# A decode block on one core: the loop of four attention steps begins at step 0, with eight turns, and what the first turn lacks stands in branches on a register

## The chip, the core and the metric

The kernel runs on one core of one Trainium2 chip. The metric is the device time of one execution in microseconds (us). Three runs of the kernel before gave 441.86, 442.12 and 442.27 us; the median is 442.12 us.

The core has five engines with an instruction stream each: PE (TensorE, the matmuls; PEld is its weight loads), DVE (VectorE), ACT (ScalarE), POOL (GpSimd) and SP (SyncE, which here issues DMAs). The core's 16 DMA engines carry all transfers, the fetches of instructions among them.

## The reference

A batch of 8 rows of width 1024 passes an attention layer and a gated layer, each behind a modulated layer norm. All inputs are bf16.

```python
mod = (silu(c) @ w_mod).reshape(8, 6, 1, 1024)        # sa, ca, ga, sb, cb, gb
h = layernorm(x) * (1 + ca) + sa
q = h @ wq                                            # 32 heads of 128
k, v = k_cache, v_cache                               # 8 batches x 4 kv heads x 8192 x 128, each kv head for 8 q heads
x = x + ga * (softmax(q @ k.T * 128 ** -0.5) @ v) @ wo
h = layernorm(x) * (1 + cb) + sb
gate = h @ W_gate                                     # 1024 x 3584
x = x + gb * ((gate * (gate > 0)) * (h @ W_up)) @ W_down
```

The two caches hold 32 pairs (kv head, batch) of 2 MB of K and 2 MB of V each. They are most of the 185.6 MB that the kernel reads.

## The kernel before

**Stages.** First the modulation (w_mod, four blocks of 3 MB) and the query projection (wq, four blocks of 2 MB). Then 32 attention steps, one for each pair n of kv head and batch. After every eight steps the output projection of that kv head (wo, 2 MB) is added. Last come the gate and up projections and the down projection (wd).

**Transfers.** Every block of weights, K or V is one DMA that SP issues (L780) into one SBUF buffer, `ring`, which has nine slots of 2 MB and a smaller region. The list `stream` is the order; SP issues the next block as soon as PE is done with the last block that lay in the same place (`behind`, L399). SP does nothing else until the output.

**An attention step n** has eight parts j = 0..7 (loop at L676). In part j PE transposes eight 128x128 tiles of K (`slot_transpose`, L580), and DVE (even j) or ACT (odd j) copies them to SBUF (`slot_evac`, L585). In between, PE computes scores of step n, DVE, PE and ACT the softmax of step n-1 (ACT's `Exp`), PE the product with V of step n-2, and the output of step n-3 is moved out (`pv_evac` on ACT, `pv_pick` on PE, `o_evac` and `o_keep` on DVE). So the steps are a software pipeline: step 0 has none of the work on older steps, step 1 has the softmax of step 0, and so on.

**Order and waits.** `_Graph` records each engine's operations in program order, with the operations they depend on. `number` (L116) gives each operation of a step's piece a semaphore; `waits` (L133) finds what an operation must still wait for; `emit` (L157) writes an engine's program. On PE, DVE and ACT the operations of steps 4 to 31 are a loop of seven turns of four steps (`L0, LN, L1 = 4, 4, N`); steps 0 to 3 and everything else are written out straight. In `loop` (L166) a wait whose value changes from turn to turn compares with a register that is raised once a turn. Work that only every second turn has (`odd=1`: the output projection) or that differs between even and odd turns (`o_keep`) stands in a branch on a register that holds 0 or 1 in turns. The parts of SP and POOL are written out.

Of the kernel before, what the change touches and what calls it, by code (L numbers as in the profile page):

```python
# [9 lines left out]


class _Op:
    __slots__ = ("eng", "fn", "deps", "inc", "value", "idx", "sem", "semval", "chan", "turn", "pos", "odd")

    def __init__(self, eng, fn, idx):
        self.eng = eng
        self.fn = fn
        self.deps = []
        self.inc = False
        self.value = 0  # L20
        self.idx = idx
        self.sem = None
        self.semval = 0
        self.chan = (eng,)
        self.turn = None
        self.pos = None
        self.odd = None


class _Buf:  # L30
# [9 lines left out]
class _Graph:  # L40
# [7 lines left out]
    def __init__(self):  # L48
        self.prog = {e: [] for e in ("pe", "dve", "act", "pool", "sp")}
        self.bufs = {}  # L50
        self.sems = {}
        self.piece = None
        self.nth = {}
        self.turn = None
        self.step = None
        self.odd = None

    def psum(self, *keys):
        for k in keys:
# [4 lines left out]
            self.bufs[key] = _Buf()  # L64
        return self.bufs[key]

    def begin(self, piece, odd=None):
        self.piece, self.nth, self.odd = piece, {}, odd

    def op(self, eng, fn, reads=(), writes=(), deps=()):  # L70
        o = _Op(eng, fn, len(self.prog[eng]))
        if self.piece is not None:
            self.nth[eng] = self.nth.get(eng, 0) + 1
            o.chan = (eng, self.piece, self.nth[eng])
            o.turn, o.odd, o.pos = self.turn, self.odd, (self.step, self.odd) + o.chan
# [24 lines left out]
        return o  # L100
# [12 lines left out]
            b.readers = {}  # L113
        return o

    def number(self, make):  # L116
# [12 lines left out]
        for c, n in count.items():  # L129
            if n:  # L130
                self.sems[c] = make("m_" + "_".join(str(x) for x in c))

    def waits(self, o, seen):  # L133

# [22 lines left out]
    def emit(self, eng, e, turns):  # L157
        ops = self.prog[eng]
        if not turns:
            return self.plain(ops, e)  # L160
        at = [i for i, o in enumerate(ops) if o.turn is not None]
        self.plain(ops[:at[0]], e)
        self.loop(eng, ops[at[0]:at[-1] + 1], e, turns)
        self.plain(ops[at[-1] + 1:], e)

    def loop(self, eng, ops, e, turns):  # L166
        by = [[o for o in ops if o.turn == k] for k in range(turns)]
        assert sum(len(b) for b in by) == len(ops)

        body, rest = [], list(by[1])  # L170
        for o in by[0]:
            while o.odd is None and rest[0].odd is not None:
                body.append(rest.pop(0))
            body.append(rest.pop(0) if o.odd is None else o)
        body += rest
        at = {}
        for k, b in enumerate(by):
            assert [o.pos for o in b] == [o.pos for o in body if o.odd in (None, k % 2)]
            seen = {}
            for o in b:  # L180

                for s, v in self.waits(o, seen if o.odd is None else dict(seen)):
                    at.setdefault(o.pos, {}).setdefault(id(s), (s, {}))[1][k] = v

        kinds = [lambda k: k, lambda k: k // 2, lambda k: (k + 1) // 2]
        regs = {}

        def value(vs, alone):
            k0, k1 = min(vs), max(vs)
            if vs[k0] == vs[k1]:  # L190
                return None, vs[k0]
            for i in (0, 2, 1) if alone else (0, 1, 2):
                t = kinds[i]
                by_, left = divmod(vs[k1] - vs[k0], max(1, t(k1) - t(k0)))
                first = vs[k0] - by_ * t(k0)
                if left == 0 and all(v == first + by_ * t(k) for k, v in vs.items()):
                    assert first > 0
                    return (i, by_, first), 0
            raise AssertionError(vs)

        plan = {}
        for pos, d in at.items():
            for s, vs in d.values():
                r, v = value(vs, pos[1] is None and all(k % 2 for k in vs))
                if r is not None and r not in regs:
                    regs[r] = e.alloc_register("%s_%d_%d_%d" % (eng, *r))
                    e.reg_mov(regs[r], r[2])
                plan.setdefault(pos, []).append((s, v if r is None else regs[r]))
        kind = [[r for r in regs if r[0] == i] for i in range(3)]
        odd = kind[1] or kind[2] or any(o.odd is not None for o in body)  # L210
        if odd:
            turn = e.alloc_register(eng + "_turn")
            e.reg_mov(turn, 0)

        def one(o):
            for s, v in plan.get(o.pos, ()):
                e.wait_ge(s, v)
            ins = o.fn(e)
            if o.inc:
# [4 lines left out]
                e.reg_add(regs[r], regs[r], r[1])  # L224

        with e.Fori(0, turns):
            if kind[2]:
                with e.If_eq(turn, 1):
                    add(kind[2])
# [11 lines left out]
            if kind[1]:  # L241
                with e.If_eq(turn, 1):
                    add(kind[1])
            add(kind[0])
            if odd:
                e.reg_mul(turn, turn, -1)
                e.reg_add(turn, turn, 1)


def bass_adaLN_cond__gqa_block_cached__glu_gated_reglu__decode_kernel(  # L250
# [25 lines left out]
    N = G * B  # L276
# [11 lines left out]
    with ExitStack() as es:  # L288
# [372 lines left out]
            dve("tensor_tensor", out=yR[:], in0=Y, in1=yR[:], op=ALU.add, reads=[pY, "yR"], writes=["yR"])  # L661


        def run(fn, *args, odd=None):
            g.begin("%s_%d" % (fn.__name__, j), odd)
# [8 lines left out]
        g.begin(None)  # L674

        for n in range(N + 4):  # L676
            g.turn = (n - L0) // LN if L0 <= n < L1 else None
            g.step = (n - L0) % LN
            wg = (n - 11) // B if n >= 11 and (n - 11) % B == 0 else None
            for j in range(8):  # L680
                if n < N:
# [6 lines left out]
                if 0 <= n - 3 < N:  # L688
# [3 lines left out]
                        run(pv_pick, n - 3)  # L692
                    elif j == 2:
                        run(o_evac, n - 3)
                        run(o_keep, n - 3, odd=(n - L0) // LN % 2)
                if 0 <= n - 2 < N and j % 2 == 1:
                    run(pv, n - 2, j // 2)
                if wg is not None and j in (4, 6):
                    run(wo_part, wg, 2 * j - 8, 2 * j - 4, odd=1)
                if wg is not None and j == 6:  # L700
                    run(wo_add, odd=1)
                if n >= 10 and (n - 10) % B == 0:
                    if j == 3:
                        run(re_turn, ot2[:].rearrange("p h r b -> p (h r b)"), "ot", odd=1)
                    elif j == 4:
                        run(re_spread, odd=1)
                    elif j == 6:
                        run(re_rows, otR[:], "otR", odd=1)
                if 0 <= n - 1 < N:
                    if j == 1:  # L710
                        run(soft_max, n - 1)
# [72 lines left out]
        g.number(lambda name: E(nc.semaphore(name)))  # L784

        block_ = E(nc.Block())
        engs = {"sp": (nc.sync, block_.sync), "act": (nc.scalar, block_.scalar), "pool": (nc.gpsimd, block_.gpsimd),
                "dve": (nc.vector, block_.vector), "pe": (nc.tensor, block_.tensor)}
        for name, (e, starter) in engs.items():
            def body(_, name=name, e=e):  # L790
                g.emit(name, e, (L1 - L0) // LN if name in LOOPED else 0)
                if name == "sp":
                    for o in last:
                        e.wait_ge(o.sem, o.semval)
# [29 lines left out]
```

## Time and profile before

| what | value |
|---|---|
| median of three runs | 442.12 us |
| the profiled execution | 442.3 us |
| its span in the profile | 440.5 us |
| PE, DVE, ACT busy | 75%, 44%, 41% of the span |
| bytes read, rate over the span | 185.63 MB, 421 GB/s |
| loads in the list of SP | 90 |
| instruction fetches of 16384 B (queue q8) | 11 |
| instruction fetches of 8192 B while the kernel runs (queue q14) | 5 |

The span is the time from the first to the last record of the profile; 1.8 us of the execution lie outside it. The page gives busy times by engine and in 40 slices, the DMA queues, the chain of work that ended last, and the costliest groups of instructions. The trace also holds each DMA packet with its start, its duration and its queue, and the time of every semaphore update, so that the landing of each load on each of the 16 DMA engines can be read.

### The profile page before, as it was taken

The page shows a single profiled execution, that of the slowest core. Times are in us where ns is not written, and L with a number is a line of the kernel's source. Part 1 is how long each engine was busy: PE and PEld are TensorE (multiplying, and loading weights), DVE is VectorE, ACT ScalarE, POOL GpSimd, SP SyncE. Part 2 cuts the span into 40 slices and gives each one's busy share as a digit, 9 for nine tenths or more (in the row PEclk, how much of TensorE's full clock was granted, in tenths as well). Part 3 has the DMA queues.
Part 4 walks back from the last instruction along what each step waited for, and adds up shares of the span by engine and source line. Part 5 has one row for each costly group of instructions (what it writes and reads, how often), then busy time and mean ns, then how long its engine had stood idle before and what let it go on. Part 6 is the DMA issues. An engine that isn't in the chain of part 4 may idle for free.

```text
span 440.5 us, 9704 instructions
## 1 busy us (share of the span) xinstructions
PE 329.1 (75%) x4114; PEld 203.9 (46%) x4114; DVE 193.5 (44%) x498; ACT 180.6 (41%) x235; POOL 7.5 (2%) x44
## 2 busy tenths in 40 slices
PE   1525578999888849998887599888849988753753
PEld 1102165656555526665555356555526655431221
DVE  3004044556445544554556155445544555435110
ACT  3000036566645433655654256555433645410000
POOL 1000000000000000000000000000000000000000
PEclk9998559999999997999999699999988999955755
DMA  8999999999999999999999999999999999999994
GB/s 347 435 420 430 433 430 428 427 434 427 427 430 431 431 431 431 430 431 431 430 433 433 430 431 430 434 428 431 433 430 431 431 431 434 426 427 431 426 428 183
DMA packets 13456, 185.87 MB, mean 422 GB/s; under 512 B 1488, under 2 KB 1520, under 8 KB 1920
## 3 DMA queue, kind: packets, MB, share of 16 engines
q1 hardware_dynamic: 13376, 185.61, 98.7%
q8 instruction: 11, 0.18, 0.1%
q10 hardware_dynamic: 64, 0.04, 0.1%
q14 instruction: 5, 0.04, 0.0%
HBM read 185.63 MB, written 0.02 MB: 421 GB/s over the span
## 4 chain that ended last, share of the span: by engine, by line
DMA 69%; PE 23%; DVE 4%; issue 2%; ACT 1%; SPq 1%; ACTq 0%
DMA ring<-in_A_k_cache_dram 48%; PE PS L424 13%; DMA ring<-in_A_wq_dram 11%; PE PS L420 10%; DMA ring<-in_B_W_down_dram 9%; SPq L780 1%; DVE pt L428 1%; DVE ov L428 0%; ACT ov L431 0%; DVE qT L428 0%; ACT pr L431 0%; DVE os L428 0%; DVE mp L428 0%; ACT L431 0%; DVE lh L428 0%
## 5 line engine op out<-in xcount | busy, mean ns | idle before, releaser
L431 ACT ACTIVATE KT<-PS 128x1024 bf16<-128x1024 bf16 (+1 forms) x132 | 133.4, 1011 | 209.6 <-PE PS L424 146.1
L424 PE MATMUL PS<-identb,ring 128*128 128x128 bf16 x2048 | 153.6, 225 | 34.0 <-DMA ring<-in_A_k_cache_dram 33.4
L424 PEld LDWEIGHTS PS<-identb,ring 128*128 128x128 bf16 x2048 | 124.6, 102 | 61.3 <-DMA ring<-in_A_k_cache_dram 43.6
L428 DVE COPY KT<-PS 128x1024 bf16<-128x1024 bf16 (+1 forms) x130 | 89.6, 689 | 131.7 <-PE PS L424 108.6
L420 PE MATMUL PS<-KT,qz 128*32 128x512 bf16 x512 | 52.8, 400 | 0.4 <-ACT KT L431 0.4
L420 PE MATMUL PS<-ring,pt 128*32 128x512 bf16 x512 | 50.8, 391 | 0.0
L428 DVE TENSOR_REDUCE mp<-PS 128x1 f32<-128x512 f32 x32 | 22.1, 692 | 8.6 <-PE PS L420 5.6
L431 ACT ACTIVATE pr<-PS,nb 128x512 bf16<-128x512 f32 x32 | 22.0, 687 | 7.1 <-DVE nb L428 6.5
L424 PE MATMUL PS<-identf,ov 128*128 128x128 f32 x128 | 22.8, 305 | 1.5 <-ACT ov L431 1.4
L428 DVE COPY pt<-PS 128x512 bf16<-128x512 bf16 x32 | 13.5, 423 | 22.0 <-PE PS L424 22.0
L420 PE MATMUL PS<-ring,siluT 128*8 128x512 bf16 x96 | 10.9, 625 | 14.1 <-DMA ring<-in_w_mod_dram 14.1
L431 ACT ACTIVATE ov<-PS 128x512 f32<-128x512 f32 x32 | 18.9, 592 | 3.9 <-PE PS L420 3.9
L420 PEld LDWEIGHTS PS<-KT,qz 128*32 128x32 bf16 x512 | 13.2, 93 | 14.7 <-issue 1.2
L424 PEld LDWEIGHTS PS<-identf,ov 128*128 128x128 f32 x128 | 14.6, 150 | 10.1 <-issue 6.1
L420 PEld LDWEIGHTS PS<-nm,rsel 8*128 8x128 f32 x64 | 9.4, 182 | 16.9 <-DVE nm L428 16.0
L420 PE MATMUL PS<-lh,onesf 128*128 128x8 f32 x64 | 12.4, 266 | 6.2 <-DVE lh L428 5.9
L420 PEld LDWEIGHTS PS<-ring,pt 128*32 128x32 bf16 x512 | 13.4, 95 | 5.9 <-issue 5.7
L420 PEld LDWEIGHTS PS<-lh,onesf 128*128 128x128 f32 x64 | 9.5, 188 | 12.3 <-DVE lh L428 12.3
L424 PEld LDWEIGHTS PS<-identb,pr 128*128 128x128 bf16 x128 | 7.2, 97 | 15.3 <-ACT pr L431 14.0
L420 PE MATMUL PS<-ring,h2T 128*8 128x512 bf16 x112 | 10.7, 500 | 4.8 <-DMA ring<-in_B_W_up_dram 3.1
L420 PE MATMUL PS<-nm,rsel 8*128 8x1 f32 x64 | 12.1, 256 | 2.9 <-DVE nm L428 2.7
L424 PE MATMUL PS<-identb,pr 128*128 128x128 bf16 x128 | 12.7, 222 | 2.0 <-ACT pr L431 2.0
(96 smaller groups left out, 171.0 us busy)
## 6 DMA issues: line engine op xcount, KB each, us to landing
ring<-in_A_k_cache_dram SPq DMA_DIRECT2D x32, 2048.0 KB, 31.8
ring<-in_A_v_cache_dram SPq DMA_DIRECT2D x32, 2048.0 KB, 27.3
ring<-in_w_mod_dram SPq DMA_DIRECT2D x4, 3072.0 KB, 20.3
ring<-in_A_wq_dram SPq DMA_DIRECT2D x4, 2048.0 KB, 42.4
ring<-in_A_wo_dram SPq DMA_DIRECT2D x4, 2048.0 KB, 34.3
ring<-in_B_W_gate_dram SPq DMA_DIRECT2D x4, 1792.0 KB, 37.1
ring<-in_B_W_up_dram SPq DMA_DIRECT2D x4, 1792.0 KB, 37.0
ring<-in_B_W_down_dram SPq DMA_DIRECT2D x3, 2048.0 KB, 40.3
```

What stands on the lines that cost most here:

```text
L420: return pe(lambda e: e.matmul(out_, lhsT, rhs, start=start, stop=stop, skip_group_check=True), reads, writes, block, deps)
L424: return pe(lambda e: e.matmul(out_, in_, ident, start=True, stop=True, is_transpose=True), reads, writes, block)
L428: return g.op("dve", lambda e: getattr(e, name)(*args, **kw), reads, writes)
L431: return g.op("act", lambda e: e.activation(*args, **kw), reads, writes)
L780: o.fn = (lambda e, o=o, d=place[key], s_=src: e.dma_start(d, s_).then_inc(o.sem, 16))
```

## The change

The loop begins at step 0 and has eight turns; the four steps that were written out are gone from the programs of PE, DVE and ACT. The place of an operation in the loop's body is now its step, its part and its piece in a fixed list (`order`). For each place `plan` notes the turns that have it. What all turns have is written plainly; the rest stands in branches on a second register, `par`, which is 0 in the first turn and then 1, 2, 1, 2, ...: "not the first turn" is `par != 0`, odd turns `par == 1`, even turns without the first `par == 2`. A register that a wait compares with is never zero: where its first value would be, the semaphore starts higher, by increments that POOL makes ahead of its own work (`bump`). The `memset` of the second half of `ot` on POOL is dropped.

```diff
-    L0, LN, L1 = 4, 4, N
+    LN = 4
...
+        low = {}
+        for eng in looped:
+            for _, s, (_, by, first) in self.plan(eng, turns)[1]:
+                if first < 1:
+                    low[id(s)] = (s, max(low.get(id(s), (s, 0))[1], by))
...
+        def when(ks):
+            if ks == set(range(turns)):
+                return None
+            if ks == odd | even:
+                return e.If_ne(par, 0)
+            if ks == odd:
+                return e.If_eq(par, 1)
+            if ks == even:
+                return e.If_eq(par, 2)
+            assert ks == even | {0}
+            return e.If_ne(par, 1)
...
         with e.Fori(0, turns):
...
             i = 0
             while i < len(body):
-                which = body[i].odd
-                if which is None:
-                    one(body[i])
-                    i += 1
-                    continue
-                with e.If_eq(turn, which):
-                    while i < len(body) and body[i].odd == which:
-                        one(body[i])
-                        i += 1
+                ks = body[i][1][1]
+                j = i
+                while j < len(body) and body[j][1][1] == ks:
+                    j += 1
+                c = when(ks)
+                if c is None:
+                    for pos, (o, _) in body[i:j]:
+                        one(pos, o)
+                else:
+                    with c:
+                        for pos, (o, _) in body[i:j]:
+                            one(pos, o)
+                i = j
...
-            if odd:
-                e.reg_mul(turn, turn, -1)
-                e.reg_add(turn, turn, 1)
+            e.reg_mod(par, par, 2)
+            e.reg_add(par, par, 1)
...
-        pool(lambda e: e.memset(ot2[:, 1], 0.0), writes=["ot"])
...
         for n in range(N + 4):
-            g.turn = (n - L0) // LN if L0 <= n < L1 else None
-            g.step = (n - L0) % LN
+            g.turn = n // LN if n < N else None
...
+        raised = [_Op("pool", lambda e, s=s, v=v: e.sem_inc(s, v), 0) for s, v in g.bump]
+        g.prog["pool"] = raised + g.prog["pool"]
```

What the built programs hold, by engine (a matmul counts as two instructions, a weight load and a matmul; with f32 operands as four):

| engine | before | after |
|---|---|---|
| PE, all | 2996 | 2258 |
| PE, ahead of the loop / loop / behind it | 1271 / 988 / 737 | 495 / 1026 / 737 |
| PE, conditional branches | 7 | 18 |
| DVE, all / conditional branches | 261 / 14 | 227 / 21 |
| ACT, all / conditional branches | 117 / 2 | 97 / 6 |
| ACT, loads of the activation table, all / in the loop | 4 / 0 | 5 / 2 |
| POOL, semaphore instructions | 33 | 58 |

The two table loads in ACT's loop were put there when the program was built: one ahead of the copy `ov<-PS` of the turn's first step, inside its branch, and one behind that branch, ahead of the first copy `KT<-PS`. Ahead of the loop the load for `Exp` is gone.

More of the change, by code (lines that the diff above doesn't have):

```diff
@@ L12 @@
 class _Op:
[L13 removed]
+    __slots__ = ("eng", "fn", "deps", "inc", "value", "idx", "sem", "semval", "chan", "turn", "pos")
     def __init__(self, eng, fn, idx):
@@ L74, in op @@
             o.chan = (eng, self.piece, self.nth[eng])
-            o.turn, o.odd, o.pos = self.turn, self.odd, (self.step, self.odd) + o.chan
+            if self.turn is not None:
+                o.turn, o.pos = self.turn, self.place + (self.nth[eng],)
         self.prog[eng].append(o)
@@ L114, in dma, with number @@
         return o
-    def number(self, make):
+    def number(self, make, turns, looped):
         ops = [o for p in self.prog.values() for o in p]
@@ L131, in number @@
                 self.sems[c] = make("m_" + "_".join(str(x) for x in c))
+        low = {}
[3 more added lines that the diff above has]
+                    low[id(s)] = (s, max(low.get(id(s), (s, 0))[1], by))
+        raised = lambda s: low.get(id(s), (s, 0))[1]
+        for o in ops:
+            o.value += raised(self.sems.get(o.chan))
+            o.semval += raised(o.sem)
+        self.bump = list(low.values())
     def waits(self, o, seen):
@@ L162, in emit @@
         self.plain(ops[:at[0]], e)
-        self.loop(eng, ops[at[0]:at[-1] + 1], e, turns)
+        self.loop(eng, e, turns)
         self.plain(ops[at[-1] + 1:], e)
[L166 to L178, printed above, removed]
-            seen = {}
[L180 to L188, printed above, removed]
+    KINDS = (lambda k: k, lambda k: k // 2, lambda k: max(0, (k - 1) // 2))
@@ new lines, in plan @@
+    def plan(self, eng, turns):
+        body, at = {}, {}
+        for k in range(turns):
+            ops = [o for o in self.prog[eng] if o.turn == k]
+            assert [o.pos for o in ops] == sorted(o.pos for o in ops)
+            for o in ops:
+                body.setdefault(o.pos, (o, set()))[1].add(k)
+        every = {p for p, (_, ks) in body.items() if len(ks) == turns}
+        for k in range(turns):
+            seen = {}
+            for o in self.prog[eng]:
+                if o.turn == k:
+                    for s, v in self.waits(o, seen if o.pos in every else dict(seen)):
+                        at.setdefault((o.pos, id(s)), (s, {}))[1][k] = v
+        waits = []
+        for (pos, _), (s, vs) in at.items():
@@ L189, in value @@
             k0, k1 = min(vs), max(vs)
             if vs[k0] == vs[k1]:
[L191 to L208, printed above, removed]
-        kind = [[r for r in regs if r[0] == i] for i in range(3)]
-        odd = kind[1] or kind[2] or any(o.odd is not None for o in body)
@@ L211, in loop @@
-        if odd:
[L212 to L216, printed above, removed]
+                waits.append((pos, s, (None, 0, vs[k0])))
+                continue
+            for i in (0, 2, 1) if k0 % 2 else (0, 1, 2):
+                t = self.KINDS[i]
+                by, left = divmod(vs[k1] - vs[k0], max(1, t(k1) - t(k0)))
+                first = vs[k0] - by * t(k0)
+                if left == 0 and all(v == first + by * t(k) for k, v in vs.items()):
+                    waits.append((pos, s, (i, by, first)))
+                    break
+            else:
+                raise AssertionError((pos, s, vs))
@@ new lines, in plan, with loop, one @@
+        return sorted(body.items()), waits
+    def loop(self, eng, e, turns):
+        body, waits = self.plan(eng, turns)
+        regs, plan = {}, {}
+        for pos, s, r in waits:
+            if r[0] is not None and r not in regs:
+                regs[r] = e.alloc_register("%s_%d_%d_%d" % (eng, *r))
+                assert r[2] > 0
+                e.reg_mov(regs[r], r[2])
+            plan.setdefault(pos, []).append((s, r[2] if r[0] is None else regs[r]))
+        kind = [[r for r in regs if r[0] == i] for i in range(3)]
+        turn = e.alloc_register(eng + "_turn")
+        par = e.alloc_register(eng + "_par")
+        e.reg_mov(turn, 0)
+        e.reg_mov(par, 0)
+        odd, even = set(range(1, turns, 2)), set(range(2, turns, 2))
+        def when(ks):
[9 more added lines that the diff above has]
+            return e.If_ne(par, 1)
+        def one(pos, o):
+            for s, v in plan.get(pos, ()):
@@ L226, in loop @@
         with e.Fori(0, turns):
-            if kind[2]:
-                with e.If_eq(turn, 1):
-                    add(kind[2])
+            if kind[1]:
+                with e.If_eq(par, 2):
+                    add(kind[1])
             i = 0
             while i < len(body):
-                which = body[i].odd
-                if which is None:
-                    one(body[i])
-                    i += 1
-                    continue
-                with e.If_eq(turn, which):
-                    while i < len(body) and body[i].odd == which:
-                        one(body[i])
-                        i += 1
-            if kind[1]:
-                with e.If_eq(turn, 1):
-                    add(kind[1])
+                ks = body[i][1][1]
[6 more added lines that the diff above has]
+                        one(pos, o)
+                else:
+                    with c:
+                        for pos, (o, _) in body[i:j]:
+                            one(pos, o)
+                i = j
+            if kind[2]:
+                with e.If_eq(par, 2):
+                    add(kind[2])
             add(kind[0])
-            if odd:
-                e.reg_mul(turn, turn, -1)
-                e.reg_add(turn, turn, 1)
+            e.reg_mod(par, par, 2)
+            e.reg_add(par, par, 1)
 def bass_adaLN_cond__gqa_block_cached__glu_gated_reglu__decode_kernel(
@@ L790, in body @@
             def body(_, name=name, e=e):
-                g.emit(name, e, (L1 - L0) // LN if name in LOOPED else 0)
+                g.emit(name, e, N // LN if name in LOOPED else 0)
                 if name == "sp":
```

29 lines of the change are left out of this document (15 added, 14 removed).

## The prediction

> **What bounds the kernel now.** I read the slices first: is a resource full all the time?
>
> ```profile
> PE   1525578999888849998887599888849988753753
> ...
> DMA  8999999999999999999999999999999999999994
> GB/s 347 435 420 430 433 430 428 427 434 427 427 430 431 431 431 431 430 431 431 430 433 433 430 431 430 434 428 431 433 430 431 431 431 434 426 427 431 426 428 183
> ```
>
> The DMA engines are busy in every slice, PE is not. Then the chain's last pieces, which say whether the end hangs on a transfer:
>
> ```profile
> 394.03 40.34 DMA ring<-in_B_W_down_dram
> 434.37 0.04 issue
> 434.41 2.76 PE PS L420 x47
> 437.17 0.02 issue
> 437.19 0.44 DVE pr L428
> 437.63 0.02 issue
> 437.65 0.42 DVE pt L428
> ```
>
> It does: PE starts the last blocks when a transfer lands and needs 2.76 us. The waits show the same over the attention steps:
>
> ```profile
> PEld PS L424 <- DMA ring<-in_A_k_cache_dram: 43.6, 21, 5.4
> ```
>
> PE waits for K 21 times, so it keeps up. From the trace's semaphore updates I listed the 90 loads: from load 8 on a 2 MB load lands each 4.84 to 4.88 us, nearly to the end. The shortest time between issue and landing after the start is 20.29 us (the V load issued at 358.85). A queue in order needs 4.87 us of that, so PE could be 15.4 us late before a DMA engine lacks work. PE's own delays do not move the end; the rate of the DMA engines does.
>
> So I looked at what else they carry.
>
> ```profile
> q1 hardware_dynamic: 13376, 185.61, 98.7%
> q8 instruction: 11, 0.18, 0.1%
> q10 hardware_dynamic: 64, 0.04, 0.1%
> q14 instruction: 5, 0.04, 0.0%
> ```
>
> By bytes the instruction fetches are nothing. But a load has landed when the slowest of 16 engines is done, and each fetch sits on one engine. I followed the packets engine by engine (undisturbed, a packet starts 4 ns before the end of the one ahead). The q8 fetches come at 30.05, 62.06, 73.34, 86.12, 96.20, 105.19, 116.08, 125.97, then 384.98, 412.46 and 432.30 us: one for each 227 to 315 PE instructions, none in turns 2 to 7. Each makes its engine later for good, measured against the least late one:
>
> ```
> fetch   1          2          3          4          5          6          7       8
> us      .28->1.70  .07->1.49  .42->1.84  .43->1.86  .18->1.66  .05->1.47  0->1.38  .13->1.55
> ```
>
> These are eight different engines, about 1.42 us each. (The 8 KB fetches add up to 0.84; two of them take one engine from .31 to 1.95.) So the latest engine is 1.95 us behind up to 384 us. Fetch 9 takes an engine from 1.67 to 3.17, fetch 10 one from about 1.5 to 3.02, fetch 11 one from about 1.8 to 3.3: the places that fetches 1, 2 and 3 had left (1.66, 1.45, 1.80). The ninth comes back to the first one's engine. At the last load the first engine is done at 433.33 and the last at 436.68, 3.34 us later; at the last 2 MB block of wd the gap is 3.56.
>
> **The change part by part.**
>
> *Fewer PE instructions.* PE's program shrinks by 2996 - 2258 = 738 instructions. Between fetches 1 and 8 PE executed 1836 instructions, 262 a fetch: 738 are 2.8 fetches, and 2258 / 262 = 8.6, so 8 remain. Behind the loop 737 stand as before; the three fetches there began 94, 352 and 630 executed instructions behind the loop, and 738 is 48 short of three times 262, so they come a little later, as numbers 6, 7 and 8 instead of 9, 10 and 11. They fall on engines not hit before, and none is hit twice. The latest engine then is the one of the 8 KB fetches, 1.95 to 2.0 behind. Last load: 3.34 - 1.97 = 1.37 us earlier (435.31). Last 2 MB wd block: 3.56 - 2.0 = 1.56 earlier (432.81). PE's end is the later of 432.81 + 2.77 = 435.58 and 435.31 + 0.46 (now 437.14 against 436.68) = 435.77. Now it is 437.14: **-1.37 us**. Bounds: nothing, if the fetches hit other engines than I think, and -1.9, if the 8 KB fetches shrink too (1.4 instead of 1.95).
>
> *Table loads.* One lies on PE's path now, between a K copy and the Exp:
>
> ```profile
> 70.18 1.02 ACT L431 ACTIVATE KT<-PS 128x1024 bf16<-128x1024 bf16 x1 [1.10 <-PE PS L424]
> 71.22 1.28 ACT L431 ACT_TABLE_LOAD   x1
> 72.52 0.69 ACT L431 ACTIVATE pr<-PS,nb 128x512 bf16<-128x512 f32 x1
> ```
>
> It goes; the loop has one in turn 0 and two in each of seven turns, 15, so 14 more: 14 x 1.28 = 17.9 us of ACT, which is idle for over half of the span. In a turn the copy of `ov` is 1.28 late and the second K copy up to 2.56, and behind it PE's scores. Cover: two turns last 82.6 us (17 loads), in which PE's weight loads wait 13.4 us for K (10.8 from 129.6 to 176.2 us, 2.6 from there to 212.3, by the waits of those windows). *Branches:* PE has 11 more in a turn. The records of `COMPARE_BRANCH` on PE take 0.06 to 0.23 us, 2.5 us at most; DVE's seven more at 0.06 make 0.4. Together at most 2.56 + 2.5 + 0.4 = 5.5 a turn, 11 in two turns, under 13.4. In the last turn the waits for K are only some 2.6 us, so attention may end up to 3 us later. Behind it PE waits 3.1 for up and 1.1, 3.1 and 3.5 for wd, 10.8 in all, and 9.4 when the loads land 1.4 earlier: cost nothing. A lag over 9.4 at that point would reach the end, less the 9.4.
>
> The Trainium skill ("ScalarE: Activation LUTs", What ACT_TABLE_LOAD costs) counts 2.66 us for a switch to a different set, 1.38 of it a drain. The rows show 0.02 us between the load and the Exp, no drain. By the skill's figure a turn would cost 2 x 2.66 + 2.9 = 8.2, an estimate, 16.4 in two turns against 13.4 of waits: 3 us more lag in each pair, 12 at the end of the attention. That is rival C.
>
> *POOL.* 58 - 33 = 25 semaphore raises now precede its first memset. Two such instructions start 0.08 us apart (0.534, 0.613): 2.0 us. `identf` is ready at 3.9 instead of 1.92, DVE's first work, 1.95 to 5.61, ends at 7.6, and PE cannot start before 8.05, when x lands. If it were more: PE then waits 3.9 us for the second mod block, and the first load that waits for PE is issued at 14.26 and lands 43.7 us later. Nothing.
>
> *Issue.* SP's list is the same; turn 0 runs the same steps with more branches and one table load in ACT's idle 5.95 us ahead of its first K copy.
>
> **The rivals.**
>
> A. *The fetches fall badly*: a ninth within the tail, or an order in which a later one returns to an engine already hit. For: the recurrence after eight is seen three times only, and the counts leave some 50 instructions of doubt. Against: three of three. Then one engine is still near 3.1: -0.2 to -0.5, 441.8.
>
> B. *Slower: the loop is fetched anew each turn.* Its body has 1026 instructions instead of 988, and 11 more jumps; if it is not kept, 4 fetches in each of seven turns fall on eight engines, 3.5 each, 3.5 x 1.42 = 5.0 us later than the main case: 445.8. It decides once the body outgrows what PE keeps. Against: not one fetch between 125.97 and 384.98, six turns of 988; 38 more is 4%. The Trainium skill ("Runtime: NRT & Kernel Launch", Instruction fetch mechanics) holds that a taken branch out of a window of two blocks forces a fetch, which would give this, but also gives PE room for 2048 instructions. The silent q8 in turns 2 to 7 agrees with the second.
>
> C. *Slower: PE falls behind by more than the cover*, because a turn's table loads and branches cost more than the 6.7 us (13.4 / 2) that its waits give back, say 8.3: attention ends 8 x 1.6 = 13 us later, 9.4 are covered, 3.6 reach the end: 444.3. Against: it needs half as much again as my upper bound of 5.5.
>
> **How the numbers follow.** The profiled execution has 442.30 us, 0.18 over the median of 442.12; I apply the difference to the median: 442.12 - 1.37 = 440.75. Chances: main case 0.62 (440.2 to 441.2), A 0.27, B 0.06, C 0.05. A measurement of this kernel tells about 0.2% (0.9 us) from no change. The main case is faster: 0.62; A is within: 0.27; B and C are slower: 0.11. The range holds main and A: 440.2 to 442.0.
>
> **What would show it.** Eight q8 fetches, none between the first turn and the tail; the last load's first and last engine about 2.0 us apart instead of 3.34, landing near 435.3; K loads still 4.85 apart; ACT with 18 table loads of 1.28, 23 us; PE's waits for K shorter but present; the waits for wd in the tail still there. Fetches in every turn would be B, a gap between loads or a tail without waits C, a spread of 3 us with eight or nine fetches A.

## The result and the profile after

The changed kernel took 440.82 us (median of nine runs, 440.71 to 440.95); the kernel before, beside it, 441.97 us (nine runs, 441.84 to 442.27). The ratio is 0.9972, 95% interval 0.9963 to 0.998: faster by 1.15 us in the medians, 0.26%. The profiled execution took 440.88 us with a span of 439.1; before it was 442.3 with 440.5.

The slices of the page after, first:

```profile
PE   1525669989788849898888599988858899754834
...
DMA  8999999999999999999999999999999999999995
GB/s 352 437 413 431 433 433 426 429 430 433 431 430 430 430 432 431 431 430 431 431 431 434 430 430 434 433 430 431 430 430 431 433 430 431 427 434 429 425 426 225
```

Nothing has changed in kind: the DMA engines are full in every slice. Only the last slice differs clearly: 225 GB/s instead of 183. The end is tidier; that is where the time came from. The DMA queues (packets, MB, share of the 16 engines' time):

```profile
q1 hardware_dynamic: 13376, 185.61, 99.0%
q8 instruction: 8, 0.13, 0.1%
q10 hardware_dynamic: 64, 0.04, 0.1%
q14 instruction: 5, 0.04, 0.0%
```

The same bytes, eight q8 fetches instead of eleven. They start at 28.98, 62.80, 71.25, 78.14, 87.63, then 382.43, 413.27 and 426.76 us: none in turns 2 to 8. The last load, followed over the 16 engines as the prediction did (when each engine is done with it, in us behind the first, sorted):

```
before   first 433.33   0 .30 .33 .48 .62 .91 1.12 1.36 1.44 1.52 1.61 1.81 1.97 2.91 3.07 3.34
after    first 433.32   0 .13 .16 .18 .71 .89  .94 1.41 1.51 1.52 1.55 1.55 1.58 1.64 1.74 1.97
```

The first engine is done at the same time as before. Before, three engines were 2.9 to 3.3 us behind, a second 1.4 us; now none is. The load lands at 435.29 instead of 436.68. The end of the chain shows what hangs on it:

```profile
394.76 38.02 DMA ring<-in_B_W_down_dram
432.78 0.04 issue
432.82 2.92 PE PS L451 x41
435.75 0.02 issue
435.77 0.43 DVE pr L459
436.20 0.02 issue
436.23 0.42 DVE pt L459
```

The last 2 MB block of wd lands at 432.78 (before 434.37), PE's last work follows at once as before, and PE ends at 435.75 (437.17). PE's waits for transfers over the whole run, and its work in the tail (start, duration, [idle before <- what ended it]):

```profile
PEld PS L455 <- DMA ring<-in_A_k_cache_dram: 40.8, 20, 5.4
```

```profile
423.03 1.05 PE L451 MATMUL PS<-ring,hmT 128*8 128x256 bf16 x32 [1.46 <-DMA ring<-in_B_W_down_dram]
427.90 1.88 PE L451 MATMUL PS<-ring,hmT 128*8 128x256 bf16 x32 [3.82 <-DMA ring<-in_B_W_down_dram]
432.82 2.90 PE L451 MATMUL PS<-ring,hmT 128*8 128x256 bf16 x48 [3.04 <-DMA ring<-in_B_W_down_dram]
```

Before, the waits for K were 43.6 us. So the work that the loop added, 14 table loads and the branches, is there and is paid out of PE's waits, which are still long. The table loads on the page, and two of them in ACT's timeline around the turn's first step:

```profile
L462 ACT ACT_TABLE_LOAD x18 | 23.1, 1283 | 2.4 <-PEq L843 1.7
```

```profile
175.34 1.02 ACT L462 ACTIVATE KT<-PS 128x1024 bf16<-128x1024 bf16 x1 [1.61 <-PE PS L455]
176.39 1.28 ACT L462 ACT_TABLE_LOAD   x1
177.68 0.60 ACT L462 ACTIVATE ov<-PS 128x512 f32<-128x512 f32 x1
178.30 1.28 ACT L462 ACT_TABLE_LOAD   x1
179.59 1.02 ACT L462 ACTIVATE KT<-PS 128x1024 bf16<-128x1024 bf16 x1
```

The `ov` copy starts 0.01 us behind the end of its load: each costs 1.28 us and nothing more.

### The profile page after: what moved, and what is told of

It reads as the page before. It is cut to its first block, busy times and chain, and to the rows that moved or that the text cites. A ratio compares the mean times of both kernels' runs of the same rounds, so it can differ in the third digit from the quotient of the medians.

```text
span 439.1 us, 10119 instructions
## 1 busy us (share of the span) xinstructions
PE 329.1 (75%) x4114; PEld 205.2 (47%) x4114; DVE 193.4 (44%) x498; ACT 199.2 (45%) x249; POOL 7.5 (2%) x43
## 4 chain that ended last, share of the span: by engine, by line
DMA 69%; PE 24%; DVE 4%; issue 1%; SPq 1%; ACT 1%; ACTq 0%
DMA ring<-in_A_k_cache_dram 49%; PE PS L455 13%; DMA ring<-in_A_wq_dram 11%; PE PS L451 10%; DMA ring<-in_B_W_down_dram 9%; SPq L812 1%; DVE pt L459 1%; DVE ov L459 0%; ACT ov L462 0%; DVE qT L459 0%; DVE mp L459 0%; DVE lh L459 0%; DVE os L459 0%; DVE KT L459 0%; ACT pr L462 0%
## 5 line engine op out<-in xcount | busy, mean ns | idle before, releaser
L455 PEld LDWEIGHTS PS<-identb,ring 128*128 128x128 bf16 x2048 | 124.1, 101 | 58.3 <-DMA ring<-in_A_k_cache_dram 40.8
L451 PE MATMUL PS<-ring,pt 128*32 128x512 bf16 x512 | 52.4, 393 | 0.0
L462 ACT ACT_TABLE_LOAD x18 | 23.1, 1283 | 2.4 <-PEq L843 1.7
L451 PEld LDWEIGHTS PS<-ring,pt 128*32 128x32 bf16 x512 | 14.5, 96 | 6.6 <-issue 5.7
L455 PEld LDWEIGHTS PS<-identb,pr 128*128 128x128 bf16 x128 | 7.2, 97 | 14.0 <-ACT pr L462 12.7
L455 PE MATMUL PS<-identb,pr 128*128 128x128 bf16 x128 | 12.7, 222 | 0.7 <-ACT pr L462 0.7
```

The lines of the kernel that those rows point to most:

```text
L451: return pe(lambda e: e.matmul(out_, lhsT, rhs, start=start, stop=stop, skip_group_check=True), reads, writes, block, deps)
L455: return pe(lambda e: e.matmul(out_, in_, ident, start=True, stop=True, is_transpose=True), reads, writes, block)
L462: return g.op("act", lambda e: e.activation(*args, **kw), reads, writes)
```

## The experiments

**Theory.** The time is set by the slowest of the 16 DMA engines. A q8 fetch takes 1.42 us from one engine; fetches go to eight engines in turn. So up to eight of them cost one engine 1.42 us once, and the ninth makes one engine late a second time: a step between eight and nine fetches, and nothing for more or fewer on either side of it until the seventeenth. **Rivals:** a price for each fetch (0.4 us each: 1.15 us / 3); the executed work or the POOL, DVE and ACT part of the change, not the length of PE's program; a loop that stays only because its body is small (B); table loads that have cost some of the gain (C). All kernels are made from the changed one; "the kernel before" ran beside each set of them on the same chip (medians of 442.05 to 442.12 us), and the ratios go by that. The changed kernel did not run in these sets. The loads of K, V and all weights are the same in every one of them.

### Longer programs

`pad1`: 128 extra transposes of an 8x8 tile (256 PE instructions) written out in the modulation, ahead of the loop. `pad3`: three times as many, 128 each at k = 1, 3 and 5.

```diff
         for k in range(KD):
...
+            for _ in range(128 * {5: 1}.get(k, 0)):
+                tr(TB(1)[:, 0:B], xrow[:, 0:128], identb[0:B, 0:B], [("KT", 1), "identb"], [pT[1]])
```

> After, with 128 transposes of 8x128 (256 PE instructions) more, written out in PE's wait behind k = 5 of the modulation; their result is not used. Theory (each fetch of PE's program makes one engine 1.42 us later, the ninth returns to the first one's engine, the latest engine sets the end): 9 fetches, the ninth in the tail, last load's spread 3.1 instead of 1.97, 441.9 to 442.1 us, +1.1 on 440.82. Rival 1 (the fetches cost by their bytes, 16 KB of 186 MB): 440.85. Rival 2 (the gain came from the table load for Exp that left PE's path ahead of turn 0, or from steps 0 to 3 otherwise): 440.8.

> After, with 384 such transposes (768 PE instructions) more, 128 behind each of k = 1, 3 and 5 of the modulation: PE's program has 3026 instructions, as many as before (2996). Theory: 11 fetches, 9 to 11 in the tail, each on an engine hit before; spread 3.3, 442.0 to 442.2, as before the change. If the number of fetches alone counted, three times the price of one of them: pad1 and this one stand 1:3. Rivals 1 and 2: 440.8 to 441.0.

`pad1` took 441.93 us (ratio to the kernel before 0.9995, 0.9986 to 1.0004), `pad3` 442.12 (1.0, 0.9991 to 1.0009). The q8 row of `pad1`'s page,

```profile
q8 instruction: 9, 0.15, 0.1%
```

and eleven in `pad3`. The last load on the 16 engines:

```
pad1     first 433.25   0 .25 .31 .44 .85 .88 .89 1.44 1.60 1.63 1.65 1.67 1.74 1.81 1.93 2.94
pad3     first 433.19   0 .04 .26 .50 .87 .87 .90 1.48 1.51 1.63 1.64 1.71 1.89 3.26 3.40 3.43
```

One fetch more than eight, one engine at a second delay; three more, three engines. Where the changed kernel was 1.15 us faster than the kernel before beside it, `pad1` is 0.19 faster and `pad3` equal: the ninth fetch brings back some 1.0 us, the tenth and eleventh together 0.2. In the profiled executions the last load lands at 436.19 and 436.62 (435.29 in the changed kernel): 0.9 us for the ninth and 0.4 for the two behind it. So most of the price is the step at the ninth, and not a price for each; the rest is that the slowest of three engines is later (3.43) than the one alone (2.94).

Over the loads of `pad3` the step can be seen as it happens. Once the eighth fetch (87.65) is served, eight engines are more than 1.25 us late, and the spread stays at 1.99 to 2.05 us for 290 us. The ninth, at 382.35, takes it to 3.5 at the next load that lands.

### The same work in a short program

`ctl3`: as many transposes as `pad3`, at the same places, but in loops of eight, sixteen turns each. `short` goes to the other side: it **leaves out** the terms k = 1, 3, 5 of the modulation, query, gate and up projections, and half of the terms of the down projection in six of its column blocks.

```diff
+            if k in (1, 3, 5):
+                def again(e):
+                    one = lambda: e.matmul(TB(1)[:, 0:B], xrow[:, 0:128], identb[0:B, 0:B], start=True, stop=True, is_transpose=True)
+                    with e.Fori(0, 16):
+                        for _ in range(8):
+                            one()
+                    return one()
+                pe(again, [("KT", 1), "identb"], [pT[1]])
```

```diff
-        for k in range(KD):
+        for k in (0, 2, 4, 6, 7):
...
-                for i in range(i0, i1):
+                for i in [i for i in range(i0, i1) if c_ == 6 or (c_ + i) % 2 == 0]:
```

> After, with the same 384 transposes (and three more) executed in the same three places, but in a loop of 16 turns of 8 in each place, so that PE's program grows by some 66 instructions instead of 768. Theory: 8 fetches, 440.8 us, spread 2.0. If PE's additional work itself cost the time in the kernel with 768 more, this one would cost the same: 442.1.

> After, shortened: the rows k = 1, 3 and 5 of the modulation, of wq and of gate and up are left out of the sums, and half of the terms of the down projection in its first six column blocks; all loads remain. PE's program has 1958 instructions instead of 2258: 7 fetches. Theory: seven engines are still delayed by one fetch each, the latest stays where it is: 440.7 to 440.9, no gain. Rival (each fetch has a price, 1.15 us for three): 440.4. Rival 2 (the end is PE's work): faster by a us or more.

`ctl3` took 440.77 us (ratio 0.9972; eight fetches, last load's spread 1.72 us) although PE executes three matmuls and as many weight loads more than in `pad3`. So it is the program's length, not the work. `short` has 1958 PE instructions, seven fetches, a spread of 1.91 and also took 440.77 (0.9971): below eight there is nothing more to be had by this road, since the crowd at 1.4 to 1.9 stays as long as one fetch of 1.42 us remains. Both are equal to the changed kernel within what the runs can tell.

| PE instructions | q8 fetches | engines hit twice | time, us |
|---|---|---|---|
| 1958 (`short`) | 7 | 0 | 440.77 |
| 2258 (the change) | 8 | 0 | 440.82 |
| 2324 (`ctl3`) | 8 | 0 | 440.77 |
| 2514 (`pad1`) | 9 | 1 | 441.93 |
| 2996 (the kernel before) | 11 | 3 | 441.97; 442.12 beside `pad1`, `pad3`, `ctl3` |
| 3026 (`pad3`) | 11 | 3 | 442.12 |

### Sixteen and seventeen fetches

If eight engines are hit in turn, 16 fetches should cost as much as 11, and the 17th one step more. `pad8` and `pad9` have eight and nine pieces of 128 transposes in the modulation, two or three at each of k = 1, 3, 5 (2,048 and 2,304 PE instructions more).

```diff
+            for _ in range(128 * {1: 2, 3: 3, 5: 3}.get(k, 0)):
+                tr(TB(1)[:, 0:B], xrow[:, 0:128], identb[0:B, 0:B], [("KT", 1), "identb"], [pT[1]])
```

> After, with 1024 transposes of 8x128 (2048 PE instructions) more, written out behind k = 1, 3 and 5 of the modulation. 16 fetches. Theory (a fetch delays one engine, the ninth returns to the first one's engine): sixteen fetches put two on each of the same eight engines, so the latest is where the one with 11 fetches has it: spread 3.4, 442.1 to 442.3. Rival (each further fetch costs, or there is no return after eight): from 11 to 16 fetches 5 x 0.45 us or one further delay of 1.4: 443.5 to 444.4. If PE's work of some 27 us more were not covered: later still, with gaps between loads.

> After, with 1152 such transposes (2304 PE instructions) more: 17 fetches. Theory: the seventeenth is the third one on the first engine; if it comes before the last loads, spread 4.4 to 4.8 and 443.2 to 443.5, about 1.1 to 1.3 over the kernel with 16 fetches. Rival (a steady price by fetch): 0.1 to 0.45 over the kernel with 16.

451.58 and 455.42 us: both times missed, by theory and by rival. They had the right number of fetches, 16 and 17. The expectation of `pad8` names work of PE that is not covered, with gaps between loads, only as a possibility, and that is what came. PE's timeline in `pad8` shows a cost that I had not put in:

```profile
26.61 3.57 PE L455 MATMUL PS<-identb,KT 8*128 8x8 bf16 x128 [0.53 <-issue]
33.36 3.57 PE L455 MATMUL PS<-identb,KT 8*128 8x8 bf16 x128 [3.18 <-issue]
39.84 2.85 PE L455 MATMUL PS<-identb,KT 8*128 8x8 bf16 x101 [2.90 <-issue]
```

128 transposes take 3.57 us and then PE stands, waiting for nothing that the profile shows. In this stretch the fetches start at 24.27, 30.94, 37.43, 44.05, 50.17, 57.15, 63.24, some 6.5 us apart. As I read it, PE runs short instructions faster than a block of 16 KB arrives behind the loads. `ctl3` agrees: there the same transposes stand in a loop, 129 of them take 5.88 us, and PE goes on without a pause. The modulation is done late, so the slots of its blocks come free late: the K load that is number 11 in the list is issued at 68.23 us instead of 36.39, with no load left ahead of it, and lands 8.26 us after the one before instead of 4.84. Another such gap, 9.31 us, comes at load 15. So these two tell nothing of the seventeenth fetch.

`sp8` and `sp9` have about as many instructions, in pieces put where PE waits anyway: ahead of the first transposes, in the modulation and the query projection, in a branch of the loop, and ahead of the down projection (`sp9`: one piece more at the start). The two pieces in the branch run in four turns, so PE executes 3,584 instructions more in `sp8`, not 2,048.

```diff
+        def few(n):
+            def body(e):
+                one = lambda: e.matmul(X[:, 288:292].bitcast(bf16), identb[0:8, :], identb[0:8, 0:8], start=True, stop=True, is_transpose=True)
...
+            pe(body, ["identb"], [pX])
...
+            if k in (1, 3, 5):
+                few(128)
...
+                if j == 7 and n % (2 * LN) == LN + 2:
+                    run(few, 256)
...
+        few(128)
```

> After, with eight pieces of 256 PE instructions more (transposes whose result is not used), as many as in the kernel that came to 451.58, but spread over PE's waits: one ahead of x's transposes, three in the modulation, one in wq, two in a branch of the loop that odd turns take, one ahead of the down projection. 16 fetches. Theory (fetches fall on the same eight engines in turn): two on each, the latest engine where 11 fetches have it, spread 3.3 to 3.6, 442.1 to 442.4. Rival (no return after eight, or a price by fetch): a spread near 2.0 with more engines delayed, or 443.5. If PE's additional work is not covered here either, gaps between loads and a later time, and the run tells nothing on the fetches.

> The same with one piece more ahead of x's transposes: 17 fetches. Theory: the seventeenth is the third on the first engine; if it is served before the last loads, spread 4.5 and 443.2; if it comes with the last ones, as before the kernel with 16: 442.1 to 442.5. Rival (a price by fetch): 0.1 to 0.4 over the kernel with 16.

The pieces hold the same small transposes. As times both missed: 448.65 us and 453.19 (the latter with runs from 447.99 to 455.58). In `sp8` PE comes late to the end: its gate projection begins at 422.86 us instead of 407.90, 15 us later, where the waits behind it give back 9.6. The piece ahead of the down projection adds 3.2. The last two fetches start at 435.94 and 439.93 us, when the last loads land and behind them, and the chain's end has PE's work in the place of the wait for a load:

```profile
434.83 3.23 PE PS L496 x126
438.23 4.86 PE PS L451 x112
443.11 0.43 DVE pr L459
443.57 0.42 DVE pt L459
```

But the transfers of `sp8` can be read by themselves: the first engine is done with the last load at 433.24, as in the kernel before (433.33), so no load had run dry. The last load landed at 436.55 (436.68 before), with 14 fetches started by 427.84 us (the fifteenth, at 435.94, comes when only the latest engines are still at work):

```
sp8      first 433.24   0 .02 .23 .24 .63 .85 .95 1.44 1.63 1.85 3.04 3.06 3.12 3.21 3.24 3.32
```

Fourteen on eight engines in turn are six engines hit twice and two once. Six stand above 3.0; of the three between 1.4 and 1.9 I take the third for the one that the 8 KB fetches keep late. Seven engines are never hit. By the landings a second hit on six engines costs no more than on three: 436.55 with fourteen fetches, 436.62 and 436.68 with eleven. The next edge, at 17, was not reached cleanly. `sp9`, where PE was late at several places, adds nothing to this.

### The table loads

`exp_ahead` has one small `Exp` on ACT ahead of the loop. With that table already loaded when the loop begins, the built program has four loads and none in the loop. `sq4` does the contrary: a `Sqrt` of 128x8 values in each step, so that ACT's table changes nine times a turn.

```diff
+        act(sig[0:B, 0:8], identb[0:B, 0:8], ACT.Exp, reads=["identb"], writes=[("KT", 2)])
```

```diff
+        def other_table():
+            act(stat[:, 2, :], stat[:, 3, :], ACT.Sqrt, reads=["stat3"], writes=["stat2"])
...
+                if j == 0 and n < N and n % LN in (0, 1, 2, 3):
+                    run(other_table)
```

> After, with one Exp of 8x8 on ACT ahead of the loop, which puts its table load there and takes both table loads out of the loop: 4 loads instead of 18, 18 us less on ACT. Theory: ACT's lag is covered, 440.8 us within 0.2, PE's waits for K some us longer. Rival 3 (the change gained 1.15 us although the table loads gave some of it back): faster than 440.82 by some tenths to 2 us.

> After, with a Sqrt of 128x8 on ACT in each of a turn's four steps, whose result is not used: 9 table loads in a turn instead of 2, 7 x 1.28 + 4 x 0.2 = 9.8 us more on ACT a turn, one load ahead of Exp and one behind it in most steps. It takes the cover away that the prediction counted on. Theory: a pair of turns has some 12 us of waits for K to give; 19.6 more, if PE feels all of it, leaves 7 to 8 us of lag a pair, 30 at the end of the attention, against 9.4 of waits behind it: 15 to 25 us slower than 440.8, and gaps between the loads in the last steps. If ACT's idle time takes up half of it: no change, 440.8.

`exp_ahead` took 440.88 us, no different from the changed kernel. Its groups of instructions and its waits show what went and where it went to:

```profile
L462 ACT ACT_TABLE_LOAD x4 | 5.1, 1283 | 1.7 <-PEq L844 1.7
```

```profile
PEld PS L455 <- DMA ring<-in_A_k_cache_dram: 44.8, 23, 5.4
```

18 us less of ACT became 5.6 us less of waiting for `ov` (4.1 instead of 9.7 by PE's weight loads), 4.0 us more of waiting for K and some 1.7 us of waiting for an up block behind the attention (3.5 instead of 1.8), and none of it reached the end. `sq4` took 447.26, between its two expectations; neither was met. Its table loads and the largest waits of PE's weight loads for ACT:

```profile
L462 ACT ACT_TABLE_LOAD x74 | 94.9, 1283 | 3.2 <-PEq L848 1.7 <-issue 0.2
```

```profile
PEld PS L455 <- ACT ov L462: 45.1, 32, 1.6
...
PEld PS L455 <- ACT pr L462: 35.3, 32, 1.4
```

In the changed kernel these two are 9.7 and 12.7, 58.0 us less. The waits for K (40.8) and for wd and up in the tail (11.6) are gone from `sq4`: the cover of 52 us is used up, and then the loads run dry. The shortest time from issue to landing falls to 8.15 us at load 74, which lands 9.15 us after the one before it instead of 4.85: 4.3 us lost for good. Of the 6.4 us over the changed kernel, 4.5 are in the landing of the last load (439.82 against 435.29) and the rest in PE's work behind it: it ends at 442.07, 2.25 us after that landing instead of 0.46. So a table load is free here as long as PE waits for K, and what ends the cover is a load with nothing ahead of it.

### The loop itself

`jump`: the loop's body has 1,100 more PE instructions that never run, in a branch that is jumped over each turn, between two transposes. The body has 2,132 instructions, PE's program 3,364. `pe_only`: only PE loops; DVE and ACT are written out for all 32 steps (597 and 309 instructions).

```diff
+        def skipped():
+            def body(e):
...
+                never = e.alloc_register("pe_never")
+                e.reg_mov(never, 0)
+                with e.If_ne(never, 0):
+                    for _ in range(550):
+                        one()
+                return full()
+            pe(body, ["identb"], [pX])
...
+                if j == 7 and n < N and n % LN == 2:
+                    run(skipped)
```

```diff
-    LOOPED = ("pe", "dve", "act")
+    LOOPED = ("pe",)
```

> After, with 1100 PE instructions in the loop's body that no turn executes (a branch jumps over them): the body has 2132 instructions instead of 1026, the program 3364. It asks for rival B of the prediction, a loop that is fetched anew in each turn. Theory: if PE keeps the body, 13 fetches at most, 442.1 to 442.3 (or 8 to 9 and 440.8 to 442.0, if what is jumped over is not fetched). If the body is too large to be kept: q8 fetches in every turn, up to 8 a turn, 1.4 us on each engine a turn, 445 to 455, more if PE waits for them.

> After, with only PE's part as a loop; DVE and ACT are written out (DVE 597 instructions instead of 227, ACT 309 instead of 97), so there are no table loads in ACT's steps and no branches on DVE. Theory: PE's fetches stay at 8; four to five more fetches of 8 KB, each 0.5 to 0.8 us on one engine: 440.8 if they fall beside PE's, up to 441.8 if two meet on an engine that PE's hit. Rival (the loops of DVE and ACT cost something themselves): faster than 440.8.

`jump` took 442.15 us (ratio 1.0004). It has nine q8 fetches: seven up to 99.12 us instead of five, two in the tail, at 400.95 and 425.53, instead of three. There are none from 99 to 400 us, while the loop passes the jump some seven times (a turn is 41 us). Its last load has one engine at 2.96 and the others at 1.74 or less, the picture of `pad1`, and nearly `pad1`'s time (I had put 442.0 at most for nine fetches). So the 1,100 instructions cost one fetch more in all, not the four that 1,100 / 262 gives, and the loop is not fetched anew even with a jump that wide in it. Rival B is not seen. A loop that executes as many as 2,132 instructions a turn was not run.

`pe_only` took 443.14 us (1.0025, 1.0016 to 1.0035), slower than the kernel before; I had expected at most 441.8. PE's program and its eight q8 fetches are those of the changed kernel. The row that differs:

```profile
q14 instruction: 10, 0.08, 0.0%
```

```
pe_only  first 433.23   0 .04 .24 .33 .91 1.01 1.43 1.49 1.66 1.68 1.72 1.78 1.78 1.88 2.01 4.38
```

One engine is 4.4 us late, the rest 2.0 or less. Over the loads it grows by steps: 1.9 up to load 44, 2.9 at load 45 (two fetches, at 236.37 and 238.48), 3.7 at load 61 (315.62), 4.5 at load 78 (396.32), while the second latest stays at 1.8 to 2.3. The last load lands 2.32 us later than in the changed kernel (437.61), and that is the whole difference in time. So 8 KB fetches can take 0.9 to 1.0 us from an engine, and at least three of the ten fell on the one that was already latest. Which engine they are sent to was not tried further.

## Why the prediction was right

The time (440.75 forecast, 440.82 measured) and the way to it agree. The range, 440.2 to 442.0, held rival A too; what tells the two apart is the last load's spread, 1.97 us and not near 3. Point by point:

- *DMA rate as the bound, PE's lag harmless.* Shown: 18 table loads or 4 give the same time; the bound held until `sq4` had used up the waits. The shortest time from issue to landing after the start fell from 20.29 to 18.78 us; that load is issued at 360.16 instead of 358.85, so PE is some 1.3 us later there, and it costs nothing. (The 4.84 to 4.88 us between landings hold for most loads; five of those up to load 75 lie outside, at 4.75 to 5.16.)
- *A fetch takes 1.42 us from one engine, and the ninth comes back to the first.* Read from three recurrences in one trace; that a second round falls on engines already hit is now shown by `pad1`, `pad3`, `jump` and the landings of `sp8`, and the doubt behind rival A is gone. That the ninth's engine is just the first one's stays a reading of places.
- *2.8 fetches fewer, eight remain.* Eight. The three of the tail came behind the loop as numbers 6, 7 and 8, but not "a little later": at 382.43, 413.27 and 426.76 instead of 384.98, 412.46 and 432.30, two of them earlier. Nothing hangs on that, since each falls on an engine not hit before. The spread at the last load was put at 1.97 and is 1.97; to the second digit that is luck, since eight fetches give 1.72 in `ctl3` and 1.99 in `exp_ahead`. Landing 435.31 put, 435.29 measured; wd 432.81 and 432.78; PE's end 435.77 and 435.75.
- *-1.37 us.* The profiled executions differ by 1.42 us, the medians by 1.15. The median of the kernel before was 442.12 in the three runs that were given and 441.97 in the nine beside the change, which hold these three; that is most of the difference.
- *Table loads and branches, at most 5.5 us a turn.* Too high. All table loads of the loop together took 4.0 us of the waits for K (44.8 in `exp_ahead`, 40.8), 0.5 a turn, and 1.7 us behind the attention: the rest, as I read it, falls into time in which nobody waited for ACT. PE's branch records grew from 7.4 to 16.2 us, 1.1 a turn and not 2.5. With the branches, the waits for K fell from 43.6 to 40.8 and the one for up from 3.6 to 1.8: 0.6 us a turn. As a bound it did its work; as a measure of the cover left it was nine times too careful. The gate projection begins at 407.90 us instead of 407.18, 0.7 later, where up to 3 was allowed. The tail's waits were put at 9.4 us and are 1.30 + 1.46 + 3.82 + 3.04 = 9.6.
- *A drain at each table load.* The Trainium skill ("ScalarE: Activation LUTs", What ACT_TABLE_LOAD costs) counts 1.38 us of drain besides the load. No run shows it: the load is 1283 ns, starts as little as 0.02 us behind the activation ahead, and the next `ACTIVATE` starts 0.01 to 0.02 us behind it, in `sq4` too, where the table really changes between Sqrt's and Exp's. Rival C needed a turn to cost 8.3 us and is not seen; by `sq4` its mechanism is real, but it needs some 50 us more of waiting for ACT.
- *The loop fetched anew (B).* Not in the changed kernel, and not with a jump over 1,100 instructions in its body. The sentence of the Trainium skill that speaks for it ("Runtime: NRT & Kernel Launch", Instruction fetch mechanics: a taken branch out of a window of two blocks forces a fetch) is not borne out: turns 2 to 8 of the changed kernel jump back over 1,026 instructions without a fetch, and in `jump` some seven turns jump over 1,100 as well.
- *POOL's 25 raises, SP's order.* Nothing, as forecast: POOL's first `memset` of its own work comes 2.0 us later (2.69 instead of 0.73), and the first engine is done with the last load at 433.32 instead of 433.33.

What the prediction had not seen lies outside the change: that written-out short instructions seem to run no faster than they are fetched (`pad8`), and that the 8 KB fetches of DVE and ACT can pile up on one engine (`pe_only`). Looping DVE and ACT, which the kernel before did already, is worth over 2 us here (443.14 against 440.82), with the engines on which these fetches happened to fall.

No version was clearly faster than the changed kernel (`ctl3` and `short`: 440.77). What is left of the spread, 1.4 to 2.0 us, is, as I read it, the first hit on each engine and the 8 KB fetches; no run took that away.

## What to carry to other kernels

When the DMA engines are full in every slice, look at when each of the 16 engines is done with the last loads: a load has landed when the slowest one is done, and a few small transfers that fall on the same engine cost more than their bytes. Count instruction fetches and ask where they fall, not how many there are: here the eighth cost nothing and the ninth about 1 us. Here the loop was free because what it adds to ACT and PE is shorter than PE's waits for transfers; read that cover from the waits before and, after, check that it is still there.

## What the runs showed of the hardware

- A q8 fetch of 16 KB is a packet of 0.88 to 0.96 us before and after the change but makes its engine about 1.42 us late. The fetches go to eight of the 16 engines in turn: with fourteen (`sp8`), six engines were hit twice and two once as the landings read, and seven show no delay of that kind.
- In `pad8`, with the DMA engines full, a fetch of 256 instructions started about each 6.5 us; 128 transposes of 8x8 took 3.57 us, 28 ns each, and PE then stood for up to 3.5 us.
- In `jump` a stretch of 1,100 instructions that is jumped over in each turn cost one fetch more in all.
- In `pe_only` an 8 KB fetch of the q14 queue took up to 1.0 us from its engine, three times the 0.31 us of its packet.
- An `ACT_TABLE_LOAD` took 1283 ns, and the next activation started 0.01 to 0.02 us behind it, also in `sq4`, where the table changes nine times a turn.
